# Retention scores in two buffers, chunk sums in one bank, running states in two operations

## The chip, the cores and the metric

The kernel runs on one core of a Trainium2 chip. The metric is the time of one execution on the device in microseconds (us), the median of several runs. Engines are called by their names or by the profile's short ones: TensorE (PE; its weight loads are PEld), VectorE (DVE), ScalarE (ACT), GpSimd (POOL) and SyncE (SP), which here only issues transfers between HBM and SBUF.

## What is computed

Retention (linear attention with decay) over 4 batches, 8 heads, 576 positions and 64 features of a head, followed by two feed-forward layers:

```python
scores = (1 / np.sqrt(64)) * np.matmul(q, k.transpose(0, 1, 3, 2))
gamma = 1.0 - 2.0 ** (-5.0 - np.arange(H))
rel = pos[:, None] - pos[None, :]
ret = scores * np.where(rel >= 0, gamma[:, None, None] ** rel, 0.0)
x = np.matmul(ret, v)                      # (4, 8, 576, 64), then (2304, 512)
g, val = x @ w_gate, x @ w_val             # 512 -> 1536
x = (g / (1 + np.exp(-g)) * val) @ w_out   # 1536 -> 512
out = np.maximum(x @ w_in, 0) ** 2 @ w_out2  # 512 -> 2048 -> 512
```

## The kernel before

The program has two stages. The first is retention and takes the first 81 us. The second holds the two feed-forward layers, as Strassen-like products of split numbers; it is nine tenths of the time and is not touched.

Retention works on 16 pairs: one batch and two heads, which lie in the two halves of the 128 partitions (`rs`). A pair's 576 positions are NC = 5 chunks: four of 128 and a last one of 64. Scores are only formed inside a chunk. What earlier chunks contribute goes through states: for each of the first four chunks a 64 x 64 sum of keys times values, and running states made from them by the recurrence "decay times the state before, plus this chunk's sum".

For pair n the program does this:

- `load_qk(n)`, `load_kv(n)`: SP's queue brings `qk_sb`, `k_sb`, `v_sb` (all five chunks of values), and for the first four pairs the mask of their heads (`mask_sb`) and a row of decays (`qs_sb`). They are issued two pairs ahead.
- `scores(n, range(4))`: 8 score matmuls 128x128 into tile `s` of two PSUM banks (one for each head), one buffer; VectorE multiplies all 1024 columns by the mask into `p_sb`.
- `scores(n, (4,))`: 2 score matmuls 64x64 of the last chunk, both heads on partitions 0 to 63, each in a bank of its own; VectorE multiplies them into `pl`, a tile whose other 64 partitions were set to 0 once.
- `states(n)`: 8 matmuls 64x64 into `kvs`, one bank with two buffers. ScalarE copies the first chunk's sum to `sb`; VectorE makes the other three states, one after another, with operations of 64 columns that read `kvs` in PSUM.
- `prep_state(n + 1)`: ScalarE scales the next keys, GpSimd scales the next queries (`qs`).
- `apply(m, False)` and `apply(m, True)` for an earlier pair m (one back at first, two back after the fourth pair): output matmuls `o` from states (`o<-qs,sb`) and scores (`o<-p_sb,v_sb`, `o<-pl,v_sb`); ScalarE copies the result to `xy`.

In each pair PE's order is: `s` of the pair, the four-chunk output of the earlier pair, the last chunk's `s`, `kvs`, the last chunk's output. All engines run their instructions in the program's order in this stage (`Chained` ties each to the one before). Between its retention operations VectorE also does work for the second stage: it decodes 64-bit weights (`words`: the rows `w<-w`, `w<-raw,w`) and splits operands (`wi`, `wb`, `xo_l`, `xs`, `xy<-xy`). `pump` and `begin` hand this out from the sixth pair on. In the second stage a scheduler sets the order.

A load on SP's or ScalarE's queue gets one of eight completion semaphores in turn, and waits until the load that had it before has landed; so at most eight are under way.

The eight PSUM banks in retention: `s` of four chunks 2, `s` of the last chunk 2, `kvs` 2, outputs 2.

Of the kernel before, what the change touches and what calls it, by code (L numbers as in the profile page):

```python
# [18 lines left out]
NP = H // 2  # L19
DM = H * D  # L20
NT = B * S
P = 128
CC = DM // P
F1 = 1536 // P
F2 = 2048 // P
NC = -(-S // P)
N = 512
M0 = 256
# [21 lines left out]

CUT = 256


# [5 lines left out]
def retention_moe_kernel(  # L59
# [319 lines left out]
    with ExitStack() as st:  # L379
# [9 lines left out]

        qk_t, k_t, v_t, q_t, p_t, sb_t = ({} for _ in range(6))  # L390
        rs = [slice(h * D, (h + 1) * D) for h in range(2)]
# [8 lines left out]
        def load_qk(n):  # L400
            b, hp = pairs[n]
            qk_t[n] = qk_p.tile([P, 2, S], F32, tag="qk", name="qk_sb")
            for at in (slice(0, CUT), slice(CUT, S)) if n == 0 else (slice(0, S),):
                sp.dma_start(out=qk_t[n][:, :, at], in_=qk[b, hp][:, :, at])

        def load_kv(n):
            b, hp = pairs[n]
            k_t[n] = k_p.tile([P, NC - 1, P], F32, tag="k", name="k_sb")
            v_t[n] = v_p.tile([P, NC, P], F32, tag="v", name="v_sb")
            queue = sp if n else act  # L410
            if n == 0:
                act.dma_start(out=ks_sb, in_=kscale)
            queue.dma_start(out=k_t[n], in_=kv[b, hp][:, NC:])
            if n < NP:
                queue.dma_start(out=mask_sb[:, n], in_=mask[:, n])
            sp.dma_start(out=v_t[n], in_=kv[b, hp][:, :NC])
            if n == 0:
                act.mul(table, one[:, :1], one[:, :1])
                load_qk(1)
            if n < NP:  # L420
                sp.dma_start(out=qs_sb[:, n], in_=qscale[:, n, P:P + qs_sb.shape[-1]])

        def prep_state(n):
# [8 lines left out]
            for c, m in ((0, 3 * P), (3 * P, D)):  # L432
# [5 lines left out]
                )  # L438
            q_t[n] = qs

        def width(c):
            return min(P, S - c * P)


        p_last = [const.tile([P, 2, 1, S - (NC - 1) * P], F32, tag=f"pl{x}", name="pl") for x in range(3)]
        for x in range(3):
            pool_e.memset(p_last[x][S - (NC - 1) * P:], 0.0)

        def scores(n, cs):

            w, nx, hp = width(cs[0]), len(cs), pairs[n][1]
            ps = ps_s.tile([P, 2, 512], F32, tag=f"s{nx}", name="s")
            for x, c in enumerate(cs):
                at = slice(c * P, c * P + w)
                for h, r in enumerate(rs):
                    pe.matmul(
                        ps[:w, h, x * w:(x + 1) * w], qk_t[n][r, 1, at], qk_t[n][r, 0, at],
                        start=True, stop=True, skip_group_check=True,
                    )
            pt = p_p.tile([P, 2, nx, w], F32, tag="p", name="p_sb") if nx > 1 else p_last[n % 3]  # L460
            dve.tensor_tensor(
                out=pt[:w], in0=ps[:w, :, :nx * w].rearrange("p h (c q) -> p h c q", c=nx),
                in1=mask_sb[:w, hp, :, None, :w].to_broadcast([w, 2, nx, w]), op=ALU.mult,
            )
            for x, c in enumerate(cs):
                p_t[n, c] = pt[:, :, x, :]

        def states(n):

            kt, vt = k_t[n], v_t[n]  # L470
            ps = ps_o.tile([P, NC - 1, P], F32, tag="kv", name="kvs", bufs=2)[:, :, :D]
            for c in range(NC - 1):
                for r in rs:
                    pe.matmul(
                        ps[r, c], kt[:, c, r], vt[:, c, r], start=True, stop=True,
                        skip_group_check=True,
                    )
            sb_t[n] = sb = sb_p.tile([P, NC - 1, D], F32, tag="sb", name="sb")
            act.copy(sb[:, 0], ps[:, 0])
            for c in range(1, NC - 1):  # L480
                dve.scalar_tensor_tensor(
                    out=sb[:, c], in0=sb[:, c - 1], scalar=qs_sb[:, pairs[n][1], -1:], in1=ps[:, c],
                    op0=ALU.mult, op1=ALU.add,
                )

        def apply(n, last):
# [8 lines left out]
            for c in (cs if last else range(1, NC - 1)):  # L495
                at = slice((c - 1) * P, (c - 1) * P + width(c))
                for r in rs:
                    pe.matmul(
                        dst(c)[r], sb_t[n][r, c - 1], q_t[n][r, at],
                        start=(c in (1, NC - 1)), stop=False, skip_group_check=True,  # L500
                    )
            for c in cs:
                pt = p_t.pop((n, c))
                for h, r in enumerate(rs):
                    pe.matmul(
                        dst(c)[r], v_t[n][:, c, r], pt[:, h, :],
                        start=False, stop=True, skip_group_check=True,
                    )
            t0 = b * S + cs[0] * P
# [29 lines left out]
        warm(WARM)  # L539
        table = const.tile([P, 1], F32, tag="table", name="table")  # L540
        mask_sb = const.tile([P, NP, 2, P], F32, tag="mask", name="mask_sb")
        ks_sb = const.tile([P, NP, NC - 1, 2, 1], F32, tag="ks", name="ks_sb")

        qs_sb = const.tile([P, NP, P + D // 2 + 1], F32, tag="qs", name="qs_sb")
        load_qk(0)
        load_kv(0)
# [6 lines left out]
        for n in range(last + 1 + LAG):  # L553
# [8 lines left out]
            if new:  # L562
                scores(n, range(NC - 1))
            fill = int(n > LOADS_FROM + 1)
# [4 lines left out]
            if new:  # L569
                scores(n, (NC - 1,))  # L570
            pump(fill)
# [346 lines left out]
```

## Time and profile before

| | us |
|---|---|
| median of 3 runs | 879.02 |
| lowest of them | 878.93 |
| the profiled execution | 879.24 |
| its span in the profile | 877.4 |
| PE busy | 867.5 (99%) |
| VectorE busy | 645.4 (74%) |
| ScalarE busy | 398.3 (45%) |
| GpSimd busy | 121.8 (14%) |

TensorE's granted clock is at full speed throughout. In the profile every instruction carries line 110, that of the helper `traced`, so instructions are told apart by the tiles they write and read: `s<-qk_sb` is a score matmul that writes tile `s` from tile `qk_sb`. A group with "x16" stands for 16 instructions; an fp32 matmul counts as two.

### The profile page before, as it was taken

To read this page: it belongs to the slowest core of one execution; us is meant where nothing else is said; L and a number is where in the kernel's file an instruction comes from. 1 tells how busy PE (TensorE), PEld (TensorE's weight loads), DVE (VectorE), ACT (ScalarE), POOL (GpSimd) and SP (SyncE) were. 2 spreads that over 40 slices of the span, in tenths; PEclk is the share of its full clock that TensorE was granted. 3 is DMA by queue.
4 is the path that set the end of the run, shared out by engine and by line. 5 is a ranking of instruction groups with operands and counts; after the bars stand their busy time and mean duration, and the time that the engine had idled before them with its cause. 6 is when DMAs were issued, how large, how long until landed. Compare 5 with 4: busy or idle time off the path is not lost.

```text
span 877.4 us, 13529 instructions
## 1 busy us (share of the span) xinstructions
PE 867.5 (99%) x5064; PEld 748.7 (85%) x5064; DVE 645.4 (74%) x1018; ACT 398.3 (45%) x709; POOL 121.8 (14%) x131
## 2 busy tenths in 40 slices
PE   9989999999999999999999999999999999999998
PEld 7877888888888888888888998989999988998987
DVE  4899899999986899677647999999534467533543
ACT  3657768565544544644324466554233233232310
POOL 2342433333130000000001311110000000000000
PEclk9999999999999999999999999999999999999999
DMA  9994757756554479888745488988676465666502
GB/s 336 402 353 158 273 203 245 254 209 228 192 174 160 146 259 370 309 276 290 270 132 188 147 305 330 351 317 307 200 240 215 126 233 202 193 206 204 167 38 72
DMA packets 75218, 203.62 MB, mean 232 GB/s; under 512 B 7696, under 2 KB 18448, under 8 KB 75152
## 3 DMA queue, kind: packets, MB, share of 16 engines
q1 hardware_dynamic: 74720, 202.34, 65.9%
q8 instruction: 40, 0.66, 0.3%
q10 hardware_dynamic: 432, 0.41, 0.1%
q14 instruction: 26, 0.21, 0.1%
HBM read 138.23 MB, written 64.49 MB: 231 GB/s over the span
## 4 chain that ended last, share of the span: by engine, by line
PE 91%; DVE 5%; DMA 1%; ACT 1%; issue 1%; POOL 0%; ACTq 0%
PE oacc L110 42%; PE g L110 26%; PE v L110 13%; PE z L110 7%; PE o L110 3%; DVE w L110 2%; PE s L110 1%; DVE p_sb L110 1%; DVE wi L110 1%; DVE xy L110 1%; DVE sb L110 1%; DMA mask_sb<-in_mask 1%; PE kvs L110 0%; DMA qk_sb<-in_qk 0%; DVE xo_l L110 0%
## 5 line engine op out<-in xcount | busy, mean ns | idle before, releaser
L110 PE MATMUL g<-xo_h,wi 128*128 128x384 f32 (+1 forms) x768 | 238.4, 364 | 0.0
L110 PE MATMUL oacc<-wo,ho_hi 128*128 128x512 f32 (+1 forms) x584 | 179.5, 388 | 0.0
L110 PEld LDWEIGHTS g<-xo_h,wi 128*128 128x128 f32 x768 | 142.3, 188 | 17.4 <-ACT cbg L110 0.2
L110 PE MATMUL oacc<-ho_hi,wo 128*128 128x512 f32 (+1 forms) x480 | 150.9, 370 | 0.8 <-DVE xy L110 0.8
L110 DVE TENSOR_TENSOR xy<-oacc,xy 128x512 f32<-128x512 f32 (+1 forms) x155 | 99.6, 648 | 59.5 <-PE oacc L110 59.0
L110 PE MATMUL g<-xo_l,wi 128*128 128x384 f32 (+1 forms) x384 | 139.6, 364 | 0.0
L110 PEld LDWEIGHTS oacc<-wo,ho_hi 128*128 128x128 f32 x584 | 108.4, 188 | 19.2
L110 PE MATMUL v<-xo_h,wi 128*128 128x512 f32 (+1 forms) x384 | 123.0, 364 | 0.0
L110 PE MATMUL oacc<-wo,ho_lo 128*128 128x512 f32 (+1 forms) x292 | 113.3, 390 | 0.0
L110 PEld LDWEIGHTS oacc<-ho_hi,wo 128*128 128x128 f32 x480 | 88.1, 188 | 17.8 <-DVE xy L110 1.5
L110 PE MATMUL oacc<-ho_lo,wo 128*128 128x512 f32 (+1 forms) x240 | 89.1, 371 | 0.0
L110 DVE TENSOR_SCALAR w<-w 128x512 f32<-128x512 f32 (+1 forms) x136 | 68.1, 503 | 17.3 <-ACT w L110 15.5
L110 PEld LDWEIGHTS g<-xo_l,wi 128*128 128x128 f32 x384 | 72.1, 188 | 8.5
L110 PEld LDWEIGHTS v<-xo_h,wi 128*128 128x128 f32 x384 | 71.2, 188 | 8.0
L110 DVE TENSOR_TENSOR cbg<-v,cbg 128x384 f32<-128x384 f32 (+1 forms) x72 | 43.0, 598 | 45.7 <-ACT cbg L110 24.3
L110 ACT ACTIVATE cag<-g 128x384 f32<-128x384 f32 (+1 forms) x36 | 19.0, 528 | 126.2 <-PE g L110 126.2
L110 PE MATMUL v<-xo_l,wi 128*128 128x512 f32 (+1 forms) x192 | 69.8, 363 | 0.0
L110 PEld LDWEIGHTS oacc<-wo,ho_lo 128*128 128x128 f32 x292 | 54.8, 188 | 11.2
L110 PE MATMUL z<-xo_h,wi 128*128 128x512 f32 (+1 forms) x192 | 62.5, 365 | 0.0
L110 ACT CAST ho_hi<-cbg 128x768 fp32r<-128x768 f32 (+1 forms) x36 | 32.7, 908 | 45.9 <-DVE cbg L110 45.7
L110 ACT ACTIVATE raw<-raw 128x512 uint32<-128x512 uint16 x68 | 46.0, 677 | 14.7 <-DMA raw<-in_w 14.6
L110 PEld LDWEIGHTS oacc<-ho_lo,wo 128*128 128x128 f32 x240 | 45.1, 188 | 8.7
(85 smaller groups left out, 1297.4 us busy)
## 6 DMA issues: line engine op xcount, KB each, us to landing
wi<-win SPq DMA_DIRECT2D x84, 512.0 KB, 4.2
raw<-in_w SPq DMA_DIRECT2D x68, 512.0 KB, 4.7
win<-wi SPq DMA_DIRECT2D x60, 512.0 KB, 3.7
wo<-wsp SPq DMA_DIRECT2D x44, 512.0 KB, 6.3
wsp<-wo SPq DMA_DIRECT2D x28, 512.0 KB, 4.7
qk_sb<-in_qk SPq DMA_DIRECT2D x15, 576.0 KB, 6.8
wst<-w SPq DMA_DIRECT2D x32, 256.0 KB, 5.8
wi<-win SPq DMA_DIRECT2D x28, 256.0 KB, 5.0
```

The lines of the kernel that those rows point to most:

```text
L110: i = op(*args, **kw)
```

## The change

The score banks are dealt out anew and with them some shapes:

- The four-chunk scores `s` get two buffers (4 banks instead of 2).
- The last chunk's scores of both heads go into one bank (1 instead of 2): head 0 on partitions 0 to 63, head 1 on 64 to 127. `pl` becomes a tile of 128 x 64, the zeroed tiles go, and the mask for it is a tile of its own, `ml_sb`, in the same layout. The last chunk's values must lie so too: they become a tile `vl`, loaded by head in two transfers, and `v_sb` is shortened from 640 to 512 columns.
- `kvs` has one buffer instead of two. ScalarE copies all four sums, to every other slot of an `sb` of eight slots (0, 2, 4, 6).
- VectorE makes the states in two operations of 3 x 64 and 2 x 64 columns out of SBUF: first sums of two neighbouring chunks into slots 1, 3, 5, then the first and second state, times the decay squared (`decay2`), added into slots 3 and 5. The states stand in slots `STATE` = 0, 1, 3, 5.
- GpSimd makes `decay2` for the first four pairs, one column each.

```diff
+        def by_head(tile_, src):
+            for h, r in enumerate(rs):
+                sp.dma_start(out=tile_[r], in_=src[h])
+
+        def load_last(n):
+            b, hp = pairs[n]
+            vl_t[n] = v_p.tile([P, D], F32, tag="vl", name="vl")
+            by_head(vl_t[n], kv[b, hp][:REST, NC - 1].rearrange("p (h d) -> h p d", h=2))
...
-            v_t[n] = v_p.tile([P, NC, P], F32, tag="v", name="v_sb")
+            v_t[n] = v_p.tile([P, NC - 1, P], F32, tag="v", name="v_sb")
...
-            sp.dma_start(out=v_t[n], in_=kv[b, hp][:, :NC])
+            if n == 1:
+                load_last(0)
+                by_head(ml_sb, mask[:REST, :, :, :REST].rearrange("p n h q -> h p n q"))
+            sp.dma_start(out=v_t[n], in_=kv[b, hp][:, :NC - 1])
+            if n:
+                load_last(n)
...
+            if n < NP:
+                pool_e.tensor_tensor(out=decay2[:, n], in0=qs_sb[:, n, -1:], in1=qs_sb[:, n, -1:], op=ALU.mult)
...
-        def scores(n, cs):
...
-            ps = ps_s.tile([P, 2, 512], F32, tag=f"s{nx}", name="s")
+        def scores(n, last):
+            hp = pairs[n][1]
+            if last:
+                at = slice((NC - 1) * P, S)
+                ps = ps_s.tile([P, 512], F32, tag="s1", name="s", bufs=1)[:, :REST]
+                for r in rs:
+                    pe.matmul(
+                        ps[r], qk_t[n][r, 1, at], qk_t[n][r, 0, at], start=True, stop=True, skip_group_check=True
+                    )
+                p_t[n, NC - 1] = p_p.tile([P, REST], F32, tag="pl", name="pl")
+                dve.tensor_tensor(out=p_t[n, NC - 1], in0=ps, in1=ml_sb[:, hp], op=ALU.mult)
+                return
+            ps = ps_s.tile([P, 2, 512], F32, tag="s4", name="s", bufs=2)
...
-            ps = ps_o.tile([P, NC - 1, P], F32, tag="kv", name="kvs", bufs=2)[:, :, :D]
+            ps = ps_o.tile([P, NC - 1, P], F32, tag="kv", name="kvs", bufs=1)[:, :, :D]
...
-            sb_t[n] = sb = sb_p.tile([P, NC - 1, D], F32, tag="sb", name="sb")
-            act.copy(sb[:, 0], ps[:, 0])
-            for c in range(1, NC - 1):
+            sb_t[n] = sb = sb_p.tile([P, 8, D], F32, tag="sb", name="sb")
+            hp = pairs[n][1]
+            act.copy(sb[:, 0:8:2], ps)
+            for scalar, at, old, new in (
+                (qs_sb[:, hp, -1:], slice(1, 6, 2), sb[:, 0:6:2], sb[:, 2:8:2]),
+                (decay2[:, hp], slice(3, 6, 2), sb[:, :2], sb[:, 3:6:2]),
+            ):
                 dve.scalar_tensor_tensor(
-                    out=sb[:, c], in0=sb[:, c - 1], scalar=qs_sb[:, pairs[n][1], -1:], in1=ps[:, c],
-                    op0=ALU.mult, op1=ALU.add,
+                    out=sb[:, at], in0=old, scalar=scalar, in1=new, op0=ALU.mult, op1=ALU.add,
                 )
```

PE's order stays row for row as it was, apart from names. SP's queue at the start of the program, before (DMAHW0 to DMAHW7 are the eight completion semaphores; the row waits for the load that had it before):

```order
L110 DMA k_sb<-in_kv 128x512 [waits DMAHW0_49]
L110 DMA mask_sb<-in_mask 128x256 [waits DMAHW1_49]
L110 DMA v_sb<-in_kv 128x640 [waits DMAHW2_49]
L110 DMA qs_sb<-in_qscale 128x161 [waits DMAHW3_49]
L110 DMA qk_sb<-in_qk 128x1152 [waits DMAHW4_49]
```

and the same place now:

```order
L114 DMA k_sb<-in_kv 128x512 [waits DMAHW0_49]
L114 DMA mask_sb<-in_mask 128x256 [waits DMAHW1_49]
L114 DMA vl<-in_kv 64x64 [waits DMAHW2_49]
L114 DMA vl<-in_kv 64x64 [waits DMAHW3_49]
L114 DMA ml_sb<-in_mask 64x4x64 [waits DMAHW4_49]
L114 DMA ml_sb<-in_mask 64x4x64 [waits DMAHW5_49]
L114 DMA v_sb<-in_kv 128x512 [waits DMAHW6_49]
L114 DMA vl<-in_kv 64x64 [waits DMAHW7_49]
L114 DMA vl<-in_kv 64x64 [waits DMAHW0_49]
L114 DMA qs_sb<-in_qscale 128x161 [waits DMAHW1_49]
L114 DMA qk_sb<-in_qk 128x1152 [waits DMAHW2_49]
```

Six small loads have come in between the second pair's mask and the third pair's `qk_sb`, and each load waits for another one than before.

VectorE's rows for the first two pairs, before:

```order
L110 TENSOR_TENSOR p_sb<-s,mask_sb 128x1024 [waits DMAHW5_49,PE_49]
L110 TENSOR_TENSOR pl<-s,mask_sb 64x128 [waits PE_49]
L110 SCALAR_TENSOR_TENSOR sb<-sb,qs_sb,kvs 128x64 [waits DMAHW7_49,Activation_49]
L110 SCALAR_TENSOR_TENSOR sb<-sb,qs_sb,kvs 128x64 [waits DVE_49] x2
L110 TENSOR_TENSOR p_sb<-s,mask_sb 128x1024 [waits DMAHW1_49,PE_49]
L110 TENSOR_TENSOR pl<-s,mask_sb 64x128 [waits PE_49]
```

and now:

```order
L114 TENSOR_TENSOR p_sb<-s,mask_sb 128x1024 [waits DMAHW5_49,PE_49]
L114 TENSOR_TENSOR pl<-s,ml_sb 128x64 [waits DMAHW5_49,DMAHW4_49,PE_49]
L114 SCALAR_TENSOR_TENSOR sb<-sb,qs_sb 128x3x64 [waits DMAHW7_49,Activation_49]
L114 SCALAR_TENSOR_TENSOR sb<-sb,decay_243 128x2x64 [waits DVE_49,Pool_49]
L114 TENSOR_TENSOR p_sb<-s,mask_sb 128x1024 [waits DMAHW1_49,PE_49]
L114 TENSOR_TENSOR pl<-s,ml_sb 128x64 [waits PE_49]
```

Nothing has changed places; the first `pl` waits for two loads more, the state operations are two instead of three and wait for ScalarE's copy and GpSimd's `decay2`.

## Rows read from the trace of the kernel before

**Rows 1.** The page's busy time of each engine, us (share of the span).
```profile
PE 867.5 (99%) x5064; PEld 748.7 (85%) x5064; DVE 645.4 (74%) x1018; ACT 398.3 (45%) x709; POOL 121.8 (14%) x131
```

**Rows 2.** Busy time by stage: stretch, its us, each engine's us (instructions), clock, DMA share.
```profile
9.30:39.00 29.70, 29.05 (x484) 24.23 (x484) 20.00 (x43) 15.48 (x40) 11.79 (x18) 1.00 1.04 398
39.00:79.30 40.30, 36.63 (x604) 29.87 (x602) 39.22 (x74) 24.30 (x62) 15.93 (x20) 1.00 0.70 260
79.30:877.40 798.10, 794.02 (x3936) 688.78 (x3932) 584.17 (x898) 356.17 (x606) 93.37 (x87) 1.00 0.65 224
```

**Rows 3.** What PE waited for up to 84 us: total us, times, longest.
```profile
PE s L110 <- DVE p_sb L110: 3.7, 5, 1.2
...
PE s L110 <- DMA qk_sb<-in_qk: 0.3, 1, 0.3
```

**Rows 4.** PE's timeline: start, us, instruction, and the idle time before it with its releaser.
```profile
25.02 1.16 PE L110 MATMUL s<-qk_sb 64*128 64x128 f32 x16 [0.45 <-DVE p_sb L110]
...
52.36 1.16 PE L110 MATMUL s<-qk_sb 64*128 64x128 f32 x16 [1.16 <-DVE p_sb L110]
...
79.07 0.87 PE L110 MATMUL o<-qs,sb 64*64 64x128 f32 x12 [0.25 <-ACT xy L110]
```

**Rows 5.** Timeline of VectorE and of GpSimd where they bear on the states.
```profile
30.05 0.68 DVE L110 SCALAR_TENSOR_TENSOR w<-raw,w 128x512 uint32<-128x512 uint32 x1
...
39.07 0.92 DVE L110 SCALAR_TENSOR_TENSOR sb<-sb,qs_sb,kvs 128x64 f32<-128x64 f32 x3 [1.45 <-ACT sb L110]
...
42.42 1.25 DVE L110 SCALAR_TENSOR_TENSOR w<-raw,w 128x512 uint32<-128x512 uint32 x1
...
77.79 0.90 DVE L110 SCALAR_TENSOR_TENSOR sb<-sb,qs_sb,kvs 128x64 f32<-128x64 f32 x3
...
42.26 1.57 POOL L110 TENSOR_TENSOR qs<-qk_sb,qs_sb 128x384 f32<-128x384 f32 x2 [2.79 <-PE o L110]
```

**Rows 6.** Groups by shape up to 84 us: count, busy us, mean ns, idle before.
```profile
L110 DVE TENSOR_TENSOR p_sb<-s,mask_sb 128x1024 f32<-128x1024 f32 x16 | 19.5, 1220 | 3.4 <-PE s L110 3.3
...
L110 DVE SCALAR_TENSOR_TENSOR sb<-sb,qs_sb,kvs 128x64 f32<-128x64 f32 x48 | 13.3, 278 | 5.4 <-ACT sb L110 3.7 <-DMA qs_sb<-in_qscale 0.6
...
L110 ACT COPY xy<-o 128x512 f32<-128x512 f32 x16 | 9.4, 586 | 22.5 <-PE o L110 22.4
...
L110 PE MATMUL s<-qk_sb 64*64 64x64 f32 x64 | 5.3, 243 | 0.0
...
L110 DVE TENSOR_TENSOR pl<-s,mask_sb 64x128 f32<-64x128 f32 x16 | 4.4, 277 | 3.0 <-PE s L110 3.0
...
L110 ACT COPY sb<-kvs 128x64 f32<-128x64 f32 x16 | 3.4, 213 | 5.6 <-PE kvs L110 3.7 <-issue 1.4 <-DVE w L110 0.3
```

**Rows 7.** The start: issue and landing (us) of the second mask; PE's first output and third pair.
```profile
4.97 0.33 SPq L110 DMA_DIRECT2D mask_sb<-in_mask  x1
...
mask_sb<-in_mask SPq DMA_DIRECT2D x1, 128.0 KB, 5.5
...
10.66 0.87 PE L110 MATMUL o<-qs,sb 64*64 64x128 f32 x12 [0.17 <-POOL qs L110]
11.46 1.09 PE L110 MATMUL o<-p_sb,v_sb 128*64 128x128 f32 x16
...
13.89 1.16 PE L110 MATMUL s<-qk_sb 64*128 64x128 f32 x16
```

**Rows 8.** DMA queues from 12 to 40 us (q1), and to 10 us (q10, ScalarE's).
```profile
q1 hardware_dynamic: 4303, 11.07, 102.8%
...
q10 hardware_dynamic: 432, 0.41, 12.0%
```

**Rows 9.** Waits behind retention: PE to the end, VectorE from 79.3 to 175 us.
```profile
PE oacc L110 <- DVE xy L110: 0.8, 2, 0.6
...
DVE wi L110 <- ACT wi L110: 1.1, 1, 1.1
DVE w L110 <- ACT w L110: 0.8, 2, 0.4
```

More of the change, by code (lines that the diff above doesn't have):

```diff
@@ L26 @@
 NC = -(-S // P)
+REST = S - (NC - 1) * P
 N = 512
@@ L388, in retention_moe_kernel @@
         ps_o = pool(st, "ps_o", 1, space=PSUM)
-        qk_t, k_t, v_t, q_t, p_t, sb_t = ({} for _ in range(6))
+        qk_t, k_t, v_t, vl_t, q_t, p_t, sb_t = ({} for _ in range(7))
         rs = [slice(h * D, (h + 1) * D) for h in range(2)]
@@ L439, in prep_state @@
             q_t[n] = qs
+            if n < NP:
+                pool_e.tensor_tensor(out=decay2[:, n], in0=qs_sb[:, n, -1:], in1=qs_sb[:, n, -1:], op=ALU.mult)
         def width(c):
             return min(P, S - c * P)
-        p_last = [const.tile([P, 2, 1, S - (NC - 1) * P], F32, tag=f"pl{x}", name="pl") for x in range(3)]
-        for x in range(3):
-            pool_e.memset(p_last[x][S - (NC - 1) * P:], 0.0)
-        def scores(n, cs):
-            w, nx, hp = width(cs[0]), len(cs), pairs[n][1]
-            ps = ps_s.tile([P, 2, 512], F32, tag=f"s{nx}", name="s")
-            for x, c in enumerate(cs):
-                at = slice(c * P, c * P + w)
+        def scores(n, last):
[11 more added lines that the diff above has]
+            ps = ps_s.tile([P, 2, 512], F32, tag="s4", name="s", bufs=2)
+            for c in range(NC - 1):
+                at = slice(c * P, c * P + P)
@@ L461, in scores @@
             dve.tensor_tensor(
-                out=pt[:w], in0=ps[:w, :, :nx * w].rearrange("p h (c q) -> p h c q", c=nx),
-                in1=mask_sb[:w, hp, :, None, :w].to_broadcast([w, 2, nx, w]), op=ALU.mult,
-            )
-            for x, c in enumerate(cs):
-                p_t[n, c] = pt[:, :, x, :]
+                out=pt, in0=ps.rearrange("p h (c q) -> p h c q", c=NC - 1),
+                in1=mask_sb[:, hp, :, None, :].to_broadcast([P, 2, NC - 1, P]), op=ALU.mult,
+            )
@@ L468, in states @@
+            for c in range(NC - 1):
+                p_t[n, c] = pt[:, :, c, :]
         def states(n):
             kt, vt = k_t[n], v_t[n]
-            ps = ps_o.tile([P, NC - 1, P], F32, tag="kv", name="kvs", bufs=2)[:, :, :D]
+            ps = ps_o.tile([P, NC - 1, P], F32, tag="kv", name="kvs", bufs=1)[:, :, :D]
             for c in range(NC - 1):
@@ L504, in apply @@
                 for h, r in enumerate(rs):
[L505 to L508, printed above, removed]
+                    a, p = (vl_t[n][r], pt[r]) if last else (v_t[n][:, c, r], pt[:, h, :])
+                    pe.matmul(dst(c)[r], a, p, start=False, stop=True, skip_group_check=True)
             t0 = b * S + cs[0] * P
@@ L540, in retention_moe_kernel @@
         table = const.tile([P, 1], F32, tag="table", name="table")
+        ml_sb = const.tile([P, NP, REST], F32, tag="ml", name="ml_sb")
         mask_sb = const.tile([P, NP, 2, P], F32, tag="mask", name="mask_sb")
@@ L544, in retention_moe_kernel @@
         qs_sb = const.tile([P, NP, P + D // 2 + 1], F32, tag="qs", name="qs_sb")
+        decay2 = const.tile([P, NP, 1], F32, tag="decay2", name="decay2")
         load_qk(0)
@@ L562, in retention_moe_kernel @@
             if new:
-                scores(n, range(NC - 1))
+                scores(n, False)
             fill = int(n > LOADS_FROM + 1)
@@ L569, in retention_moe_kernel @@
             if new:
-                scores(n, (NC - 1,))
+                scores(n, True)
             pump(fill)
```

7 lines of the change are left out of this document (4 added, 3 removed).

## The prediction

> **What bounds the kernel now.** I read the page's busy shares first: PE is busy in 99% of the span [rows 1]. Nearly nothing but PE's idle time and PE's own work can therefore be won. The busy time by stage says where PE idles [rows 2]. After 79.3 us PE has 794.02 of 798.10 us. From 9.3 to 39 us, the first half of the retention stage, it has 29.05 of 29.70. From 39 to 79.3 us it has only 36.63 of 40.30, and there VectorE is full, 39.22 of 40.30. So the stage has two regimes: PE sets the pace up to about 39 us, VectorE from there to the end of retention.
>
> The list of what PE waits for names one wait that matters: score matmuls `s` for VectorE's `p_sb`, 3.7 us in five waits [rows 3]. In the timeline these are gaps ahead of a pair's eight score matmuls; the first is 0.45 us at 25.02, the longest 1.16 at 52.36 [rows 4]. The score tile has one buffer, so pair n+1 may not write it before VectorE has read pair n. The reader should see that the other four lie in the regime where VectorE is full: a second buffer lets PE run ahead, but not past VectorE.
>
> **The change, part by part.**
>
> *Second score buffer.* PE's order is the same row for row; only the wait of `s` for VectorE goes. PE then depends on VectorE through three later points: the one bank of the last chunk's scores (matmul `s` 64x64 waits for the multiplication `pl` of the pair before), the states `sb` of two pairs back, and the evacuations. The 0.45 us at 25.02 goes whole. Of the 3.3 us behind 39 us only as much goes as VectorE finishes earlier, apart from a start that was not VectorE's: the last pair's output began at 79.07 after a 0.25 us wait for ScalarE [rows 4], while VectorE had its states ready at 77.79 + 0.90 = 78.69 [rows 5].
>
> *PE's matmuls.* The last chunk's matmuls take another shape (64 rows by 64 columns for both scores and output). The rows have that tile already: `s` 64*64 64x64 takes 243 ns [rows 6], and the outputs from states stand on a 64*64 tile too [rows 4]. Cost 0.
>
> *VectorE.* `p_sb` with 1024 elements takes 1220 ns, `pl` with 128 takes 277, so an element costs (1220 - 277) / 896 = 1.05 ns [rows 6]. `pl` has 64 elements instead of 128: 0.07 us less. A state operation with 64 elements takes 278 ns; the new ones have 192 and 128 elements, 278 + 128 x 1.05 = 412 and 278 + 64 x 1.05 = 345 ns. The three old ones take 0.90 us together, which leaves gaps of 0.03. New: 0.41 + 0.03 + 0.35 = 0.79, 0.11 less. In the full regime lie nine state groups (39.07 to 77.79) and eight `pl`: 9 x 0.11 + 8 x 0.07 = 1.5 us saved. Bounds: if each new operation cost only the 278 ns of the old one, 0.31 x 9 + 0.56 = 3.3 saved. The other bound is contention. The new operations read both tensors from SBUF, where the old ones read one from PSUM. `w<-raw,w`, the same kind of operation with both tensors in SBUF, takes 0.68 us at 30.05 and 1.25 at 42.42, while GpSimd was at work from 42.26 on [rows 5]: 1.84 times as long. Stretched so all nine times, the state groups cost 0.84 x 0.76 x 9 = 5.7 us more and the saving becomes a loss of 4.2. GpSimd is busy 15.93 of the 40.30 us [rows 2]; evenly spread that is 0.40 x 5.7 = 2.3 us. But its `qs` starts when an output of PE is done [rows 5], while the states come late in VectorE's pair: I take 0.6 us of stretching, so 0.9 us saved.
>
> *ScalarE.* The copy of the chunk sums grows from 64 to 256 elements. The rows give 213 ns for 64 and 586 for 512 [rows 6], 0.83 ns an element, so 0.37 us instead of 0.21. VectorE waited for this copy once in the full regime, 1.45 us at 39.07 [rows 5]: that start moves by 0.16. Elsewhere VectorE comes to the states after the copy. Chunk sums in one bank instead of two: the next sums come a whole pair of matmuls later, so 0.
>
> *The loads at the start.* This is what the change adds. SP's order shows two small loads `vl` for every pair, and two of `ml_sb` ahead of the second pair's `v_sb`; each load also waits for the load eight places before. The first `pl` now waits for `ml_sb`, and in VectorE's queue the first states and the second `p_sb` stand behind it. When does it land? `mask_sb` was issued at 4.97 and landed 5.5 us later, at 10.47 [rows 7]. Ahead of it the first `v_sb` is 64 KB smaller. The main queue moves 11.07 MB in 102.8% of 28 us of 16 engines [rows 8], 460 us, or 42 ns for 1 KB of one engine, so 64 KB are 0.17 us: `mask_sb` lands at 10.3. Then 640 packets of 256 bytes follow (128 of `vl`, 512 of `ml_sb`), 40 on each engine. Price of such a packet: ScalarE's queue moved 432 packets in 12.0% of 10 us of 16 engines, 19.2 us [rows 8]; 256 are the 384 KB of keys and mask, 16.1 us by bytes; the other 176 are 128 bytes or less, 18 ns each. By bytes alone 256 bytes cost 10 ns. I take 20; the upper bound is the 42 of 1 KB. So `ml_sb` lands at 10.3 + 40 x 0.020 = 11.1. `pl` ends at 11.3, the states at 11.7 and 12.1. The first output's six state matmuls run from 10.66, and its `p_sb` part starts at 11.46 [rows 7], so a third of them is 0.27 us: the last two started at 11.2, now at 12.1. Loss at the start 0.9 us; the third pair's scores, at 13.89 before [rows 7], come at 14.8. The third pair's `qk_sb` stands behind all this and `v_sb`, `vl` and `qs_sb`: at 2.6 ns a KB over 16 engines 11.1 + 0.67 + 0.16 + 0.21 + 1.5 = 13.6 us, in time.
>
> In the Trainium skill, DMA: Bandwidth & Descriptors, section Specifications, transfers need at least 512 bytes for line rate, with read-modify-write below that. No row here has a packet of 256 bytes; the 18 ns ones, smaller still, speak against a large penalty. At an estimate of twice my price by that rule `ml_sb` would land at 11.9, and the sum would be 0.8 us later.
>
> After the start it balances: `v_sb` loses 512 bytes in each of 128 rows, 8 x 21 ns = 0.17 us of every engine, and `vl` brings 128 packets, 8 x 20 ns = 0.16. The transfer engines are full up to 39 us [rows 2], but score matmuls waited only 0.3 us for `qk_sb` [rows 3]. I charge nothing.
>
> *Sum.* Start +0.9, the wait at 25.02 -0.45: +0.45 when VectorE's full regime begins, and ScalarE's copy makes it +0.6. Minus 0.9 saved there: the last states are ready at 78.69 + 0.6 - 0.9 = 78.4. The last output's third pair of state matmuls stood at 79.07 + 0.54 = 79.6 and can now go at 78.4. PE itself would be ready at about 78.0: it had 3.7 + 0.25 = 4.0 us of waits from 25 us on [rows 3, 4], loses 0.9 at the start, and I leave it some 2 us ahead of the last chunk's bank, 79.07 - 4.0 + 0.9 + 2. So retention ends 1.2 us earlier.
>
> *Does the rest keep it?* VectorE is only 0.3 us earlier there, PE 1.2. After retention PE waits just 0.8 us, for VectorE's `xy` [rows 9]; VectorE has waits for ScalarE of 1.1 + 0.8 = 1.9 us up to 175 us [rows 9] in which it can catch up 0.9. I take it as kept. The profiled execution took 879.24 us, the median is 879.02: 879.24 - 1.2 = 878.0, and 0.2 less by the median: **877.8 us**.
>
> **Rivals.**
> 1. *No change.* The double buffer only moves PE's waits from `s` to the last chunk's scores, VectorE's saving is eaten by stretching beside GpSimd, or PE's gain is given back as longer waits for `xy` near 170 us. For it: VectorE full from 39 to 79 us. Against it: the 0.45 us and the waits for ScalarE go anyway. With stretching of 1.5 us instead of 0.6: 878.7; with 2.3, 879.5.
> 2. *Slower: the small packets.* At 60 ns a packet `ml_sb` lands at 12.7, the start loses 2.5 instead of 0.9, and each pair needs 8 x 0.06 - 0.17 = 0.31 us more of full transfer engines, 2.2 over seven pairs, of which I count 1 us off, since `qk_sb` was hardly waited for. The time is 877.8 + 1.6 + 1.2 = 880.6. It decides from about 45 ns on. Against it: 18 ns for smaller packets.
> 3. *More.* The new operations cost 278 ns each and stretch nowhere: 3.3 saved instead of 0.9. The 2 us of waits that I left to PE go too, so it is ready at 76.0, and its third pair of state matmuls runs at 76.6 instead of 78.4: 877.8 - 1.8 = 876.0.
>
> On the second SBUF tensor, which the stretching hangs on, the Trainium skill (VectorE: DVE Perf Modes, section Two Vector instructions with no wait between them) says that the second read interface is shared with GpSimd; the 1.25 us row agrees.
>
> **How the numbers follow.** Forecast (876.9 to 878.6): 0.55. No change (878.6 to 879.5): 0.22. Slower (879.5 to 882): 0.13. More (875 to 876.9): 0.10. The range 876.0 to 879.8 leaves out half of the third rival and most of the second. The forecast's own range is 876.9 to 878.6. 2% of this kernel, about what a measurement can tell from no change, is 17.6 us. VectorE's worst loss, 4.2 us, stays far below it, and all of PE's idle time is 1% of the span [rows 1]. Faster by over 2%: 0.01; within 2%: 0.97; slower: 0.02.
>
> **What would show it.** The wait of `s` for `p_sb` gone, in its place waits of `s` 64x64 for `pl` of about 2 us; the first `pl` waiting for `ml_sb` until about 11.1; state operations of 0.41 and 0.35 us; the last output's state matmuls, at 79.07 now, 1.2 us earlier. It is wrong if `pl` starts beyond 12 us, if state operations beside GpSimd are common, or if the gain at 80 us is not there at 877.

## The result: slower, 884.88 us

The changed kernel takes 884.88 us (median of six runs, 884.23 to 886.42), the kernel before 878.97 beside it: a ratio of 1.0069 (95% interval 1.0059 to 1.0079). The forecast was 877.8 and its range ended at 879.8. By the measure of 2% this is still "no change", but the sign is wrong and the time lies outside the range. The profiled execution took 884.43 us, its span 882.6.

The page's busy time of the kernel after (us, share of the span, instructions) answers to [rows 1]: PE's work is the same, its share has gone from 99 to 98%.

```profile
PE 868.6 (98%) x5064; PEld 749.1 (85%) x5064; DVE 644.4 (73%) x1002; ACT 401.1 (45%) x709; POOL 122.0 (14%) x132
```

Busy time by stage of the kernel after (columns as in [rows 2]):

```profile
9.30:39.00 29.70, 25.11 (x374) 20.59 (x372) 14.76 (x27) 12.51 (x30) 9.19 (x18) 0.89 0.93 306
39.00:79.30 40.30, 37.91 (x650) 31.51 (x648) 38.89 (x65) 27.44 (x64) 17.94 (x23) 1.00 0.87 304
```

The loss is in the first line. Where PE had 29.05 of 29.70 us and the transfers ran at 398 GB/s [rows 2], PE has 25.11, at a granted clock of 0.89 in the mean of the stretch, and the transfers move 306 GB/s with their engines still 93% busy. What PE waited for up to 90 us (columns as in [rows 3]):

```profile
PE s L114 <- DMA qk_sb<-in_qk: 5.1, 6, 2.3
...
PE o L114 <- DVE sb L114: 0.9, 1, 0.9
PE s L114 <- DVE pl L114: 0.8, 2, 0.5
```

The 3.7 us for `p_sb` [rows 3] are gone, as the change wants. In their place stand 5.1 us for the scores' own load, which was 0.3. PE's timeline shows the longest of these waits, and where retention ends (the next stage's first `g`):

```profile
26.84 2.49 PE L114 MATMUL s<-qk_sb 64*128 64x128 f32 x20 [2.33 <-DMA qk_sb<-in_qk]
...
83.43 1.12 PE L114 MATMUL o<-qs,sb 64*64 64x128 f32 x12 [0.40 <-ACT xy L114]
...
85.88 0.50 PE L114 MATMUL g<-xo_h,wi 128*128 128x512 f32 x1
```

The kernel before has its first `g` here:

```profile
81.42 0.50 PE L110 MATMUL g<-xo_h,wi 128*128 128x512 f32 x1
```

The last output, at 79.07 before [rows 4], is at 83.43, 4.4 us later; the first `g` is 4.5 us later. Most of the 5.2 us by which the span grew (877.4 to 882.6) is there.

Why is `qk_sb` late? SyncE's queue (start, us that the issue took, load, count), first the third pair's `qk_sb` in the kernel before, then the kernel after:

```profile
7.35 0.33 SPq L110 DMA_DIRECT2D qk_sb<-in_qk  x1
```

```profile
6.06 1.16 SPq L114 DMA_DIRECT2D vl<-in_kv  x2
7.27 1.26 SPq L114 DMA_DIRECT2D ml_sb<-in_mask  x2
...
9.37 1.12 SPq L114 DMA_DIRECT2D vl<-in_kv  x2
10.54 0.58 SPq L114 DMA_DIRECT2D qs_sb<-in_qscale  x1
11.17 0.43 SPq L114 DMA_DIRECT2D qk_sb<-in_qk  x1
11.64 0.43 SPq L114 DMA_DIRECT2D k_sb<-in_kv  x1
...
13.07 1.11 SPq L114 DMA_DIRECT2D vl<-in_kv  x2
14.23 0.58 SPq L114 DMA_DIRECT2D qs_sb<-in_qscale  x1
14.94 0.34 SPq L114 DMA_DIRECT2D qk_sb<-in_qk  x1
...
18.47 1.11 SPq L114 DMA_DIRECT2D vl<-in_kv  x2
19.62 0.58 SPq L114 DMA_DIRECT2D qs_sb<-in_qscale  x1
20.32 0.36 SPq L114 DMA_DIRECT2D qk_sb<-in_qk  x1
```

Two `vl` loads of 16 KB hold SyncE for 1.1 us, about three times as long as one `qk_sb` of 576 KB. The six small loads ahead of the third pair's `qk_sb` take 1.16 + 1.26 + 1.12 = 3.5 us of issuing, and that load is issued at 11.17 where it was issued at 7.35. From 9.37 to 14.8 us SyncE issues with hardly a pause and is still late. The transfers from 9 to 40 us in 40 slices, GB/s, of the kernel after with its main queue (packets, MB, share of 16 engines), and then of the kernel before:

```profile
GB/s 251 137 260 79 151 262 372 371 385 307 168 292 388 388 268 228 193 232 328 334 383 407 294 363 294 118 193 291 359 419 389 391 406 373 420 381 385 335 382 385
...
q1 hardware_dynamic: 5752, 9.53, 92.4%
```

```profile
GB/s 403 414 399 393 377 379 409 369 378 385 390 397 387 383 415 412 405 371 404 413 416 389 400 416 387 417 424 379 390 408 404 426 394 382 397 420 443 381 373 401
```

Before, the transfer engines were fed all the time. After, they fall to 79 to 300 GB/s again and again up to 31 us; from there on they stay at 335 GB/s or more, though small loads are issued at 30.3 and 34.5 too.

### The profile page after: what moved, and what is told of

The parts are those of the page before. It is cut to its first block, busy times and chain, and to the rows that moved or that the text cites. A ratio compares the mean times of both kernels' runs of the same rounds, so it can differ in the third digit from the quotient of the medians.

```text
span 882.6 us, 13550 instructions
## 1 busy us (share of the span) xinstructions
PE 868.6 (98%) x5064; PEld 749.1 (85%) x5064; DVE 644.4 (73%) x1002; ACT 401.1 (45%) x709; POOL 122.0 (14%) x132
## 4 chain that ended last, share of the span: by engine, by line
PE 86%; DVE 8%; DMA 2%; issue 1%; ACT 1%; SPq 1%; POOL 0%; DVEq 0%; ACTq 0%
PE oacc L114 41%; PE g L114 25%; PE v L114 12%; PE z L114 6%; DVE w L114 3%; DVE p_sb L114 1%; DVE xy L114 1%; DVE wi L114 1%; DVE xo_l L114 1%; DVE sb L114 1%; PE s L114 1%; SPq L114 1%; PE o L114 1%; DMA qk_sb<-in_qk 1%; DMA k_sb<-in_kv 1%
## 5 line engine op out<-in xcount | busy, mean ns | idle before, releaser
L114 PEld LDWEIGHTS g<-xo_h,wi 128*128 128x128 f32 x768 | 142.3, 188 | 17.9 <-ACT cbg L114 0.8
```

The costliest lines, as they stand in the source:

```text
L114: i = op(*args, **kw)
```

## The experiments

Theory A: the added loads hold up SyncE's queue and starve the transfers. Rival B: the new operations, banks or states cost the time. Beside them: small packets as such, the chain over GpSimd, and TensorE's clock.

**The change without its loads.** The last chunk's values ride as 64 more columns on the `v_sb` load (`VW` is 4 x 128 + 64), its mask on `mask_sb`:

```
-            sp.dma_start(out=v_t[n], in_=kv[b, hp][:, :NC - 1])
-            if n:
-                load_last(n)
+            sp.dma_start(out=vv, in_=kv[b, hp][:, :VW])
```

> The changed kernel, with the last chunk's values as 64 more columns of the v_sb load and the last chunk's mask as 64 more columns of each mask_sb load (laid out so on the host). No load is added over the kernel before, no packet is small; score buffers, banks, states and multiplications are those of the changed kernel. Theory A (the added loads did it: they take SyncE's issuing time and places in the queue, the score loads come late, and the wait then drops the clock): the waits of s for qk_sb fall from 5.1 to below 1 us, PE is at full clock from 26 to 34 us, and the time is 877.0 to 878.5, near my forecast for the rest of the change. Rival B (the new operations did it: two-operation states stretched beside GpSimd, ScalarE's longer copy, one bank for two heads): 883 to 885, as the changed kernel. Rival C (only the placing of waits: the double score buffer gives nothing): 879 to 880.

879.01 us, ratio 0.9994 (0.9986 to 1.0003); again in a later comparison:

> The kernel in which vl and ml_sb ride on the v_sb and mask_sb loads, once more on the same chip beside the one with the filled wait: 878 to 879.5 with some runs near 876.5, as the first time, whichever theory holds. If its runs at a mean clock of 1.0 are again about 2 us shorter than those at 0.997 to 0.998, the clock carries the spread; if runs at 1.0 lie among the others, it does not.

878.38 us, ratio 0.9995 (0.9985 to 1.0004). So rival B falls: what is left of the change costs nothing, and it gains nothing that can be told from zero. The 879.01 lies in the range of rival C, just above the 878.5 with which theory A's range ended: the loads explain the loss, but my gain is missing. PE's waits of this kernel up to 90 us, and its timeline:

```profile
PE s L115 <- DVE pl L115: 3.5, 3, 2.1
...
PE s L115 <- DMA qk_sb<-in_qk: 0.2, 1, 0.2
```

```profile
60.03 0.33 PE L115 MATMUL s<-qk_sb 64*64 64x64 f32 x4 [2.14 <-DVE pl L115]
...
80.21 0.50 PE L115 MATMUL g<-xo_h,wi 128*128 128x512 f32 x1
...
102.76 0.50 PE L115 MATMUL g<-xo_h,wi 128*128 128x512 f32 x1 [0.59 <-ACT cbg L115]
```

The 3.7 us for `p_sb` come back as 3.5 for `pl`, and the first `g` is at 80.21 where it was at 81.42 before, 1.21 us earlier against my 1.2. Half of that goes at 102.76, where `g` waits for ScalarE's `cbg`, a wait that the kernel before has not. The chain of waits of this kernel shows what is behind it:

```profile
96.27 3.77 DMA raw<-in_w
100.04 0.41 DVE gate L115
...
101.00 0.69 ACT raw L115
101.69 0.56 ACT w L115
102.25 0.47 ACT cbg L115
```

Up to 96.27 us this chain runs on VectorE, then over a weight load and VectorE's `gate` to ScalarE, whose copy to `cbg` starts at 102.15 where it started at 102.77 before: this chain is only 0.6 us earlier.

**The loads without the change.**

```
+            if n == 1:
+                load_last(0)
+                by_head(ml_sb, mask[:D, :, :, :D].rearrange("p n h q -> h p n q"))
             sp.dma_start(out=v_t[n], in_=kv[b, hp][:, :NC])
+            if n:
+                load_last(n)
```

> The kernel before, with the 16 vl loads and the two ml_sb loads of the changed kernel issued at the same places of SyncE's queue, into buffers that nothing reads; v_sb keeps its 64 KB more per pair. Nothing else is changed. Theory A (added loads): waits of s for qk_sb of 4 to 6 us, PE at half clock for some us after the longest of them, 884 to 888, since the 3.7 us of waits for p_sb stay or are covered by the new waits. Rival B (new operations): 879 to 880.

886.77 us, ratio 1.0089 (1.0076 to 1.0102). (There are 34 added loads, not 18: each of the 17 rows in the queue is two.) The loads alone cost 7.9 us, more than the whole change (this kernel also still brings 64 KB more of `v_sb` for each pair). Its waits up to 90 us:

```profile
PE s L110 <- DMA qk_sb<-in_qk: 6.6, 5, 2.6
PE s L110 <- DVE p_sb L110: 3.1, 4, 1.2
```

Here the waits for `p_sb` stay beside those for the load; in the changed kernel they are gone. Theory A stands.

**Number of loads or their packets?** First the kernel of the loads alone again, with one row in each added load:

```
-                sp.dma_start(out=tile_[r], in_=src[h])
+                sp.dma_start(out=tile_[r][:1], in_=src[h][:1])
```

> The kernel before, with the added loads of the changed kernel at the same places of SyncE's queue (32 vl loads and two ml_sb loads in 17 pairs; an earlier expectation counted them as 18), but of one row each: one packet for a vl load instead of 64, into buffers that nothing reads. The same loads with all their rows made 886.77 us of the kernel before. If their number decides (issuing time on SyncE, about 0.55 us each, and places among the loads in flight): waits of s for qk_sb of 4 to 7 us again and 884 to 888. If their packets decide: those waits stay below 1 us and the time is 878.5 to 880. In between, 880 to 884, both have a share, and the difference to 886.77 is the packets' part.

884.18 us, ratio 1.0054 (1.0041 to 1.0067). With 40 packets instead of 2560, and practically no bytes, 5.3 of the 7.9 us are still there. But they don't come as expected of the number of loads: PE waits for `qk_sb` only 2.2 us, not 4 to 7. The line of the waits, and PE's timeline, first of the kernel before, then of this one:

```profile
PE s L110 <- DMA qk_sb<-in_qk: 2.2, 2, 2.0
```

```profile
18.21 1.16 PE L110 MATMUL s<-qk_sb 64*128 64x128 f32 x16
```

```profile
15.70 2.08 PE L110 MATMUL s<-qk_sb 64*128 64x128 f32 x16 [2.00 <-DMA qk_sb<-in_qk]
...
22.86 1.16 PE L110 MATMUL s<-qk_sb 64*128 64x128 f32 x16
```

The third pair's scores stood at 13.89 [rows 7], so one late load costs 1.8 us. After that wait PE is at a granted clock of 0.50 (1.2 of 2.4 GHz) up to 21 us, and the fourth pair's scores come 4.65 us late: the half clock costs 2.8 us more. Retention ends 4.8 us late (first `g` at 86.19), so the other 28 small loads cost practically nothing in this execution. All five runs of this kernel have a mean clock of 0.996 or 0.998, so none shows its time at full clock.

Then half as many loads with the same bytes, one transfer of 128 partitions for each `vl` and for `ml_sb`. The packets are not quite the same, other than the expectation says: the mask lies packed in HBM here, so `ml_sb` comes in 128 packets of 1 KB instead of 512 of 256 bytes. (The number of added loads is 17 instead of 34.)

```
-            by_head(vl_t[n], kv[b, hp][:REST, NC - 1].rearrange("p (h d) -> h p d", h=2))
+            sp.dma_start(out=vl_t[n], in_=kv[b, hp][:, NC - 1, :D])
```

> The changed kernel, with each pair's vl loaded by one transfer of 128 partitions instead of two of 64, and ml_sb by one instead of two: the same bytes in the same 256-byte packets, half as many added loads (9 instead of 18 over the stage). If the number of loads decides (issuing time on SyncE and places in the queue): the waits of s for qk_sb fall by half or more, 880 to 882.5. If the small packets themselves decide: no change, 884 to 885.5. If neither (rival B, the new operations): 884 to 885.5 too, with the waits for qk_sb unchanged.

881.32 us, ratio 1.0029 (1.0017 to 1.0041), with waits of 3.6 us for `qk_sb`. And no small packet, but three loads for `v_sb` instead of one:

```
+            for x in range(3):
+                at = slice(x * VW // 3, (x + 1) * VW // 3)
+                sp.dma_start(out=vv[:, at], in_=kv[b, hp][:, at])
```

> As the kernel in which vl and ml_sb ride on the v_sb and mask_sb loads (879.01 us), with each pair's v_sb load (288 KB) cut into three of 96 KB: as many loads for a pair as in the changed kernel, the same bytes, 768 bytes in a packet. If the number of loads decides: waits of s for qk_sb of 3 to 5 us and 882 to 885. If small packets decide (256 bytes): waits below 1 us, 879 to 880.5.

881.66 us, ratio 1.0031 (1.0019 to 1.0043):

```profile
PE s L115 <- DMA qk_sb<-in_qk: 5.5, 8, 1.5
```

At the same number of loads for a pair as in the changed kernel, 768-byte packets wait as long in sum, in eight shorter waits, but cost only 2.6 us over the 879.01, between the two expectations. So the number of loads costs time without small packets, but the runs give it no single share: 5.3 of 7.9 us by the one-row loads, of which 2.8 in the profile are half clock behind one wait, and 2.6 of 5.9 by this kernel.

What goes with the order of the times is SyncE. Its issue rows from 9 to 40 us, added up (an issue's time can hold a wait of its own), when it issues the third pair's `qk_sb`, and when that pair's scores begin:

| kernel | issue rows, us | `qk_sb` issued | scores begin | median, us |
|---|---|---|---|---|
| before | 14.4 | 7.35 | 13.89 | 878.9 |
| values on the `v_sb` load | 14.1 | 7.44 | 13.99 | 879.0 |
| one transfer each | 17.9 | 9.22 | 15.16 | 881.3 |
| `v_sb` in three | 21.4 | 9.21 | 14.71 | 881.7 |
| one-row loads | 20.6 | 10.57 | 15.70 | 884.2 |
| the changed kernel | 23.1 | 11.17 | 15.65 | 884.9 |
| the loads alone | 23.9 | 11.63 | 16.53 | 886.8 |

The two kernels that follow don't fit this order: with other things moved too, 24.4 us of issue rows go with 883.9 (the order of the loads) and 13.0 with 887.5 (another queue).

The Trainium skill (DMA: Bandwidth & Descriptors, section Rules for kernel authors) says that transfers under 64 KB are mostly overhead; the 16 KB loads here agree, with 0.55 us of SyncE's queue for each, where most loads of 576 KB took 0.34 to 0.43.

**Another queue.** All small loads issued by ScalarE:

```
-                sp.dma_start(out=tile_[r], in_=src[h])
+                act.dma_start(out=tile_[r], in_=src[h])
```

> The changed kernel, with all vl and ml_sb loads issued by ScalarE instead of SyncE: the same loads, bytes and packets on another queue. If SyncE's serial issuing and its queue's places make the scores late: the waits of s for qk_sb fall from 5.1 to below 1.5 us, and the time is 878 to 881 (ScalarE is busy 25 of 40 us between 39 and 79 us, so 32 issues in it may hold up its copies a little). If the transfer engines have too little time for these packets whatever the queue: waits of 3 us and more, 883 to 886.

887.46 us, ratio 1.0095 (1.0079 to 1.0111): slower still, outside both expectations. Its waits up to 90 us:

```profile
PE o L114 <- ACT xy L114: 4.4, 3, 2.1
PE kvs L114 <- ACT k_sb L114: 2.7, 1, 2.7
PE s L114 <- DMA qk_sb<-in_qk: 1.1, 1, 1.1
```

The wait for `qk_sb` falls to 1.1 us, which speaks for SyncE's queue as the place (PE, held up elsewhere, also needs these loads later); but ScalarE's own work now stands behind the loads. The mean clock of this profile, 0.990, is also the lowest of all, so part of the time is half clock. The Trainium skill (Perfetto Trace Analysis, section DMA Optimizations) says that balancing loads over the engines that can issue them may help where issuing is the bottleneck; here the wait fell and the time rose, as PE waits for ScalarE.

**The order of the loads.** `qs_sb` ahead of `v_sb` and `vl`:

```
+            if 0 < n < NP:
+                sp.dma_start(out=qs_sb[:, n], in_=qscale[:, n, P:P + qs_sb.shape[-1]])
...
-            if n < NP:
+            if n == 0:
                 sp.dma_start(out=qs_sb[:, n], in_=qscale[:, n, P:P + qs_sb.shape[-1]])
```

> The changed kernel, with the qs_sb loads of the second to fourth pair issued ahead of the pair's v_sb and vl loads instead of behind them: the same loads, bytes and packets in another order. In the changed kernel the fifth pair's qk_sb was issued at 20.32 us, behind GpSimd's qs of the third pair, which had waited for qs_sb until 19.02. If this chain over GpSimd is what made the scores late (theory A1): GpSimd's third qs starts about 2 us earlier, the wait of 2.33 us falls below 1 us, and the time is 880 to 882.5. If SyncE's issuing time and the places in its queue do it whatever the order (theory A2; SyncE was issuing without a pause up to 20.20): the sum of the waits for qk_sb stays at 4 to 6 us, 883.5 to 886.

883.93 us, ratio 1.0060 (1.0048 to 1.0072). GpSimd's third `qs` moves from 19.02 only to 18.23, the waits for `qk_sb` become six of at most 1.0 us (4.0 in sum), and the first output waits 2.0 us for `sb` instead of 0.9, since `ml_sb` is now later (`pl` starts at 12.21 instead of 11.20). The longest wait is gone and the time is nearly the same: the order only chooses who waits. The chain over GpSimd, which the trace had suggested, was shortened by 0.8 us only, so this run doesn't exclude that it has a part.

**TensorE's clock.** After the wait at 26.84 the 20 score matmuls took 2.49 us, where the same row takes 1.42 at full clock, and the granted clock of 26.5 to 39 us was 0.73. I put the cost at some 3 us and filled the waits with matmuls on ones; first eight, one pair too late (at `n == 5`), then three ahead of the fifth pair:

```
+            if n == 4:
+                warm(3)
             if new:
                 scores(n, False)
```

> The changed kernel, with eight more matmuls of 128 x 256 on ones, whose output nobody reads, ahead of the sixth pair's scores: they fill about 1.2 us or more of the 2.33 us in which PE stood before those scores. If the half clock after that wait costs about 3 us of its own (7 us of PE time at 0.5 to 0.62), keeping PE at work keeps full clock from 27 to 33 us and the time falls to 881 to 883. If the half clock costs nothing, because VectorE or the loads would have held PE in that stretch anyway: 884 to 886.

> The changed kernel, with three more matmuls of 128 x 256 on ones, whose output nobody reads, ahead of the fifth pair's scores, where PE stood 2.33 us in the changed kernel: by the 3.72 us that eight of them took, three take 1.4 us, so they lie inside the wait. If half clock after the wait adds a loss of its own (the 20 score matmuls took 2.49 us there and 1.42 in a kernel at full clock): full clock from 26.9 to 33 us, first g of the next stage 2 to 3 us earlier than the changed kernel's 85.88, 881.5 to 883. If the half clock was covered by VectorE or by loads that come late anyway: a longer wait for the next qk_sb instead, 884 to 885.5.

887.11 us (ratio 1.0093, 1.0080 to 1.0106) and 885.80 us (1.0079, 1.0065 to 1.0092). Both lie outside both of their ranges, and neither tells what it should. The eight stood behind the wait, not in it, and took 3.72 us of PE; the three wait themselves, because their bank has to be emptied by ScalarE, and end in the half clock that they were to prevent:

```profile
26.98 2.51 PE L114 MATMUL v<-one 128*128 128x256 f32 x6 [1.75 <-ACT xy L114]
29.42 2.10 PE L114 MATMUL s<-qk_sb 64*128 64x128 f32 x20
```

The changed kernel's own six runs tell more: 884.72 us at a mean granted clock of 1.0, 884.23 and 885.04 at 0.998, 884.43 at 0.996, 885.15 at 0.995 and 886.42 at 0.994. So the loss is there at full clock too, and down to 0.996 the clock makes no difference that shows; the two runs with the lowest clock are the longest. Elsewhere it does cost: 2.8 us in the profile of the one-row loads, above.

**Which part has the 1.2 us?** One score buffer with the new states, then two with the old states (ScalarE copies one chunk's sums, VectorE three operations):

```
-            ps = ps_s.tile([P, 2, 512], F32, tag="s4", name="s", bufs=2)
+            ps = ps_s.tile([P, 2, 512], F32, tag="s4", name="s", bufs=1)
```

```
-            act.copy(sb[:, 0:8:2], ps)
+            act.copy(sb[:, 0], ps[:, 0])
+            for c in range(1, NC - 1):
                 dve.scalar_tensor_tensor(
```

> As the kernel in which vl and ml_sb ride on the v_sb and mask_sb loads (879.01 us), with one score buffer instead of two: what is left of the change is the two-operation states, the one bank for the last chunk and the one bank of chunk sums. That kernel waited 3.5 us for pl in three waits (0.9, 2.1, 0.5) and had eleven runs of 876.3 to 879.6, the slower ones with a mean granted clock of 0.997 or 0.998. If the second buffer wins its 0.45 us and no more, and VectorE's savings are the gain: 877.5 to 878.5. If the second buffer only gathers PE's waits into fewer, longer ones, after which the clock sometimes falls: waits of s for p_sb of at most 1.2 us each, mean clock 0.999 to 1.0 in every run, 877 to 878.5, and less spread. If the second buffer carries the gain: 879 to 880, as the kernel before.

> As the kernel in which vl and ml_sb ride on the v_sb and mask_sb loads (879.01 us), with the states of the kernel before (ScalarE copies one chunk's sums, VectorE does three operations a pair): what is left of the change is the second score buffer, the one bank of the last chunk and the one bank of chunk sums. The counterpart with the new states and one score buffer took 878.97. By my prediction the second buffer wins 0.45 us at 25 us and the states 0.9 more, of which half is lost behind retention: 878.5 to 879.2, first g of the next stage at 81 us. If the two-operation states cost time (stretched beside GpSimd): 876.5 to 878. If they carried the gain: 879.5 to 880.5.

878.97 us (ratio 1.0004, 0.9995 to 1.0012), in none of its ranges, and 880.07 us (1.0010, 1.0001 to 1.0019), as expected if the states carry the gain. The first `g` of the first in PE's timeline, then the second's waits of PE up to 90 us and its first `g`:

```profile
80.14 0.50 PE L115 MATMUL g<-xo_h,wi 128*128 128x512 f32 x1
```

```profile
PE kvs L115 <- issue: 1.9, 1, 1.9
PE kvs L115 <- ACT xy L115: 1.9, 3, 0.7
```

```profile
81.10 0.50 PE L115 MATMUL g<-xo_h,wi 128*128 128x512 f32 x1
```

With the new states and one score buffer retention ends as early as with two (80.14 and 80.21). With the old states and two buffers it ends at 81.10, and PE waits at the one bank of chunk sums instead, 5.0 us in all its waits of `kvs`. So with the new states the second buffer gains nothing, and one bank for the sums is free only with these states. What the second buffer would gain with the old states and two banks for the sums, no run shows.

**Can the gain be kept?** Of the 22 runs of the change without its loads, seven took 876.3 to 877.2 us, all at a mean clock of 1.0. Three more at 1.0 took 878.4 to 879.1, and the twelve below 1.0 took 878.0 to 880.6: short runs come at full clock only, but full clock is not enough. Two kernels filled the waits for `pl`, the first from the bank of `warm`, the second into the next pair's score buffer (one matmul for the twelfth pair, three for the thirteenth, one for the fourteenth):

```
+                if n in FILL:
+                    s_next[n + 1] = ps_s.tile([P, 2, 512], F32, tag="s4", name="s", bufs=2)
+                    for _ in range(FILL[n]):
+                        pe.matmul(s_next[n + 1][:, 0, :256], one[:, :P], one, start=True, stop=True, skip_group_check=True)
```

> As the kernel in which vl and ml_sb ride on the v_sb and mask_sb loads (879.01 us), with five more matmuls of 128 x 256 on ones, whose output nobody reads, ahead of the last chunk's scores of the twelfth (1), thirteenth (3) and fourteenth pair (1): there PE waited 0.87, 2.14 and 0.50 us for VectorE's pl. By 0.465 us each they lie inside these waits. If the long wait is what lets the clock fall in the slower runs of that kernel (0.997 to 0.998, 878.5 to 879.6): no run below 0.999, 875.5 to 877.5, faster than both kernels. If the clock falls elsewhere: 878 to 879.5, with the same spread.

> As the kernel in which vl and ml_sb ride on the v_sb and mask_sb loads (879.01 us), with five more matmuls of 128 x 256 on ones, whose output nobody reads, in front of the last chunk's scores of the twelfth (1), thirteenth (3) and fourteenth pair (1), where PE waited 0.87, 2.14 and 0.50 us for pl. They write into the score buffer of the pair that follows, which VectorE has already read then, not into the bank that an earlier try had to wait for. If PE's long wait lets the clock fall in most runs: mean clock 0.999 or 1.0 in nearly all, most runs at 876 to 877, median 876.3 to 877.3, faster than both kernels. If the loss lies behind retention: 878.5 to 879.5, runs at full clock no faster than the others.

880.17 us (ratio 1.0018, 1.0006 to 1.0031), in neither of its ranges, and 878.95 us (1.0000, 0.9991 to 1.0009). The first had to wait for its bank:

```profile
PE v L117 <- ACT xy L117: 3.2, 1, 3.2
```

The second held the mean clock at 0.999 or more in nine of eleven runs, and these took 877.7 to 879.0: full clock alone doesn't bring the gain. But its filling has a price of its own, which no run separates (in its profile, one of the other two runs, PE waits 1.6 us for `qk_sb` and the first `g` is at 81.52). What sets the seven shorter runs apart stays open; no version here beats the kernel before by more than its interval.

## Why the prediction was wrong

Right, by its own steps:

- The wait for `p_sb` goes and waits for `pl` take its place: 0.8 us in the changed kernel, 3.5 without the added loads (I had named about 2).
- The start: `pl` waits for `ml_sb` until 11.20 (predicted 11.1), then the states take 0.41 and 0.35 us as worked out. The small packets' price was right: the trace's 2560 packets of 256 bytes took 18 ns each in the mean, where I had 20, and the first output loses 0.9 us, as I had it.

```profile
11.20 0.23 DVE L114 TENSOR_TENSOR pl<-s,ml_sb 128x64 f32<-128x64 f32 x1 [2.99 <-DMA ml_sb<-in_mask]
11.34 0.41 DVE L114 SCALAR_TENSOR_TENSOR sb<-sb,qs_sb 128x192 f32<-128x192 f32 x1
11.85 0.35 DVE L114 SCALAR_TENSOR_TENSOR sb<-sb,decay 128x128 f32<-128x128 f32 x1
```

- ScalarE's copy of four sums: 375 ns against 0.37 us. With the new states the banks cost nothing.
- Retention 1.2 us earlier: 1.21 without the added loads, but from other terms. My 1.2 held a loss of 0.9 at the start, which that kernel doesn't have, and let the second buffer bring PE ahead of VectorE; in the runs the kernel with one score buffer has 1.28 and the second buffer adds nothing. That the number agrees is luck.

Wrong:

- **"After the start it balances … I charge nothing."** This is the step that failed. I compared 0.17 us less of `v_sb` with 0.16 us more of `vl` on the transfer engines, as if they were always fed. On these engines the sum was right. But the loads had to be counted where they are issued: two more for each pair, 1.1 us of SyncE, and two more of the places among which each load waits for the one eight places before it. I named the places without a price and left out the issuing. Worth, with the same omission at the start (next point) and the half clock that followed a wait: 5.9 us in the changed kernel, 7.9 on the kernel before.
- **"13.6 us, in time."** The same step at the start: my sum had only transfers, as if the load were in the queue by then. The third pair's `qk_sb` was issued at 11.17 only, behind six small loads, and its scores began at 15.65, with 0.68 us of waiting for it; I had 14.8.
- Rival 2 had the right loads and the wrong reason: it made them slow through their packets, 60 ns each, and gave 880.6. The packets took 18 ns, and the one-row loads, 40 packets in all, cost 5.3 us.
- The stretching beside GpSimd was too small. The groups by shape of the changed kernel up to 84 us:

```profile
L114 DVE SCALAR_TENSOR_TENSOR sb<-sb,qs_sb 128x192 f32<-128x192 f32 x16 | 8.8, 553 | 4.4 <-ACT sb L114 4.4
L114 DVE SCALAR_TENSOR_TENSOR sb<-sb,decay 128x128 f32<-128x128 f32 x16 | 5.6, 352 | 0.8
```

The first operation has a mean of 553 ns where 412 were worked out: 16 x 0.14 = 2.3 us over the stage. Twelve of the sixteen took 0.41 or 0.42 us as worked out; four, each beside work of GpSimd, took 0.88 to 1.13. Two of these lie in the last nine pairs, which I had charged 0.6 us, and cost 0.9; the other two come in the pairs just before. It didn't decide: without the added loads it was 534 ns, and retention ended on time.

- **"I take it as kept."** Only half of the 1.2 us is kept to the end of the profiled execution, for the wait at 102.76; and in the medians nothing is left of it.

Open: how the loss divides between SyncE's issuing time and the places among the loads in flight. At the start it is mostly issuing time: 3.5 of the 3.8 us by which the third pair's `qk_sb` is issued later. Later SyncE also waits for loads, and no run here separates the two; the one-row loads take the same places and cost next to nothing there, which speaks against the places alone. Open too is what the half clock has of the loss in each kernel.

## What to carry to other kernels

A load has a price where it is issued, and where transfers are full that price is paid by whoever's load stands behind it: count the issues of each queue and their time from its own rows, not the bytes alone. Look first at the start, where one late load can hold up everything, and at the granted clock behind each long wait. A small operand should ride on a load that is made anyway; on this kernel that turned 884.9 us into 878.4 to 879.0. A second buffer gains nothing where the engine that empties the first one is full: the wait moves to the next single buffer.

## What had not been expected of the hardware

- An issue of 64 partitions of 256 bytes holds SyncE longer (0.55 us, half of the 1.1 us above) than most of 128 partitions of 4.5 KB (0.34 to 0.43 us for five of the seven from 9 to 40 us; the other two took 0.62 and 1.03).
- The transfer engines read as 92.4% busy at 309 GB/s, where 102.9% gave 398: the big packets take longer too (those of 4.5 KB 213 ns in the mean of the trace, 190 before), so the busy share doesn't tell that a queue is starved; GB/s does.
- The wait before a fall of the clock to half was 2.3 us at 26.84 and, in another kernel, 1.6 at 51.48, while one of 2.14 at 60.03 left the clock at 1.00 from 60 to 79 us in one profile and 0.91 in another of the same kernel. In the loads alone a wait of 2.63 at 16.53 left it at 1.00, and one of 2.04 at 35.50 was followed by 0.53. The length of one wait doesn't foretell it.
